# Two buffers of x change places in a fused attention and feed-forward kernel: which unit's x goes to the late pool

## The chip, the cores and the metric

The kernel runs on one core of one Trainium2 chip. The metric is the device time of one execution in microseconds: the median of several runs. Before the change it is 931.96 us, the median of three runs (930.52, 931.96 and 933.09). A profiled execution took 932.41 us; its span in the trace, on which all times below are counted, is 930.6 us.

## The reference

Linear attention without a softmax, a normalisation, and a feed-forward layer with a squared ReLU, all in fp32:

```python
# q, k, v: (8 batches, 8 heads, 576 rows, 64); g_norm: (64,)
kv = np.einsum('bhsd,bhse->bhde', k, v)
out = np.einsum('bhsd,bhde->bhse', q, kv)
rms = np.sqrt(np.mean(out * out, axis=-1, keepdims=True) + 1e-06)
out = out / rms * g_norm
x = out.transpose(0, 2, 1, 3).reshape(4608, 512)
# w_in: (512, 2048), w_out: (2048, 512), s and b: one number each
h = x @ w_in
r = np.maximum(h, 0.0)
g = s * (r * r) + b
return g @ w_out
```

## The kernel before, in words

**Units.** The 4608 rows of x are worked off in nine units (`u` from 0 to 8) of 512 rows. A unit has 512 rows times 512 features of x, kept transposed in one tile `xT[u]` (128 partitions, 2048 numbers each). A unit has two parts: the first product with its ReLU and square (`mm1`, four steps `s` of 512 columns of `w_in`), and the second product (`mm2`), whose results are stored. Meanwhile the attention for the next unit is done piece by piece between the matmuls: `attention_of_two` makes two blocks of 128 rows, so a unit needs two of them, `A` and `B`.

**Seven products instead of eight.** From unit 1 on, the products are done in Strassen's manner (the form of Winograd), so a block product becomes seven half-size products of sums and differences. The names `x1`, `z2`, `x6`, `y7`, `x5`, `x3`, `y4` give the bank of PSUM (x, y or z) and the number of the product. `x5`, `x3`, `x6` go on adding in the bank in which `x1` began, `y4` in the bank of `y7`. Products 1, 2 and 3 read `xT[u]` itself (`x_of`), products 4 to 7 read sums (`xs`). After `x5`, ScalarE copies the bank to r4 (`keep`), and VectorE adds y and r4 to `a22` and squares it. Product `y4` may add into its bank only when that addition has read it. `x3` and `y4` of a step come in the step after it; those of unit 1's last step (`s = 3`) come in slot 0 of `mm2(1)`, just after its first product, `x1(0)`.

**The order.** The order of the work is written out by hand, and each engine takes its instructions in this order: the tables in `sides` and `side_of` say ahead of which product, or in which slot of `mm2`, a piece of attention is put. For unit 1 the entry `(3, 2): [A["norm"], A["turn_x"]]` puts the normalisation (L584) and the transpose into `xT[2]` (L595) in the last step, ahead of `y7` and of `x5` with its addition. All matmuls of the products have the line of one helper, L91; additions and subtractions on VectorE have L251 and L254.

**The buffers of x.** `turn_x` in `attention_of_two` takes the tile for `xT[u]` from a pool when a unit's first two blocks come (`j == 0`). The pool `xp` has one buffer under this name from the beginning. The pool `late["x"]` has one more; it is made in `tc_late` at the end of unit 0, when the pool `convp`, with the weights of unit 0 and the raw tiles of their conversion, is given back, and it lies in that memory. In the kernel before, units 0, 1 and 2 all use the one buffer of `xp`; then units 3, 5 and 7 use the late one and units 4, 6 and 8 that of `xp`. A tile's first writing waits until all readers and writers of what lay there before are done; these waits are put in when the program is built. The readers of `xT[1]` are the products x1, z2 and x3 of unit 1 and the sums of unit 1's x (L254), and the last of them is x3 of the last step.

**Transfers.** SyncE issues most loads: k and v, a ring of seven buffers for weights of the second product (L789, L786, filled by `pump`) and, once, the 32 small loads of q for unit 3 (L1382). GpSimd issues the other loads of q (L1341), the stores of the output (L921) and, in `mm2(1)`, stores of sums of weights (L833, `parts_of_w`).

Of the kernel before, what the change touches and what calls it, by code (L numbers as in the profile page):

```python
# [16 lines left out]
def kernel(  # L17
# [61 lines left out]
    xp = ctx.enter_context(tc.tile_pool(name="xp", bufs=1))  # L79
# [40 lines left out]
    def parts(c):  # L120

        g, i = divmod(c, R)
        if g == 0:
            if i == 4:
                return [(0, 8, 1), (1, 8, 1)]
            b, i = (0, i) if i < 4 else (1, i - 5)
            return [(b, i, 1), (b, 4 + i, 1)]
        if i == 4:
            return [(2 * g, 16, 2), (2 * g + 1, 0, 2)]
        return [(2 * g, 4 * i, 4)] if i < 4 else [(2 * g + 1, 4 * i - 18, 4)]  # L130
# [268 lines left out]
    late, xT = {}, {}  # L399
# [12 lines left out]
    def small(name, n, i=""):  # L412
        return attp.tile([P, n], FP32, name=name, tag=f"{name}{i}")
# [85 lines left out]
    def scale_x(u, j):  # L499
        to = xT[u][:, :, j * P : j * P + 2 * P]  # L500
        for i in range(KC):
            nc.scalar.activation(to[:, i], to[:, i], AF.Copy, scale=g_col[:, i : i + 1])  # L502

    def attention_of_two(c):

        u, j = divmod(c, 4)  # L510
        by_block = []
        for i in range(2):
            p = parts(c + i)
            by_block += [p[0][0]] * 2 + [p[-1][0]] * 2
        runs = []
        for w, b in enumerate(by_block):
            if runs and runs[-1][0] == b:
                runs[-1][2] = 32 * w + 32
            else:
                runs.append([b, 32 * w, 32 * w + 32])  # L520
        W = 8
        st = {}

        def turn(i=None):
            if i in (None, 0):
                st["qT"] = attp.tile([P, 2 * DM], FP32, name="qT", tag="qT").rearrange(
                    "p (a x) -> p a x", a=NP
                )
            if i is None:
                nc.vector.transpose(  # L530
                    out=st["qT"], in_=q_tile[c].rearrange("p (a x) -> p a x", a=NP)
                )
                return
            to = st["qT"][:, :, i * P : i * P + P]
            if c + i >= R:
                nc.vector.transpose(out=to, in_=q_in[c + i])
                return
            ps = ps_t.tile([P, NP, P], FP32, name="qT_ps", tag="t")
            for p in range(NP):
                nc.tensor.transpose(ps[:, p, :], q_in[c + i][:, 2 * p : 2 * p + 2, :], ident)  # L540
            nc.scalar.copy(to, ps)

        def product():
            ps = [ps_t.tile([P, 2, 2 * P], FP32, name="y_ps", tag="t") for _ in range(2)]
            for b, lo, hi in runs:
                for r in range(2):
                    for p in range(NP):
                        for l in range(2):
                            rows = slice(l * HB, l * HB + HB)
                            at = l * HB + r * 32  # L550
                            nc.tensor.matmul(  # L551
                                ps[l][32 * p : 32 * p + 32, r, lo:hi],
                                lhsT=bd_kv[b % 2][rows, p, at : at + 32],
                                rhs=st["qT"][rows, p, lo:hi],
                                start=True,
                                stop=True,
                            )
            st["ps"] = ps

        def back():  # L560
            y = q_tile[c].rearrange("p (w l d) -> p w l d", w=W, l=2)
            for l in range(2):
                nc.vector.transpose(
                    out=y[:, :, l].rearrange("p w (r e) -> p r w e", r=2),
                    in_=st["ps"][l].rearrange("p r (w t) -> p r w t", w=W),
                )

        def square():
            st["xn"] = attp.tile([P, 2 * DM], FP32, name="xn", tag="xn")
            nc.scalar.activation(st["xn"], q_tile[c], AF.Square)  # L570

        def row_sum():
            st["ss"] = small("ss", 2 * W, 2)
            nc.vector.reduce_sum(
                st["ss"], st["xn"].rearrange("p (h d) -> p h d", d=D), axis=mybir.AxisListType.X
            )
            st["rms"] = small("rms", 2 * W, 2)
            nc.scalar.activation(st["rms"], st["ss"], AF.Sqrt, bias=eps_col, scale=1.0 / D)

        def norm():  # L580
            inv = small("inv", 2 * W, 2)
            nc.vector.reciprocal(inv, st["rms"])
            shape = (P, 2 * W, KC, D // KC)
            nc.vector.tensor_tensor(  # L584
                out=st["xn"].rearrange("p (c h e) -> p h c e", c=KC, h=2 * W),
                in0=q_tile[c].rearrange("p (h c e) -> p h c e", h=2 * W, c=KC),
                in1=inv.unsqueeze(2).unsqueeze(3).to_broadcast(shape),
                op=ALU.mult,
            )

        def turn_x():
            if j == 0:
                pool = late["x"] if u > 2 and u % 2 else xp
                xT[u] = pool.tile([P, KC, 2 * TB], FP32, name="xT", tag="xT")
            nc.vector.transpose(  # L595
                out=xT[u][:, :, j * P : j * P + 2 * P],
                in_=st["xn"].rearrange("p (c x) -> p c x", c=KC),
            )

        return dict(  # L600
            turn=turn, product=product, back=back, square=square, row_sum=row_sum, norm=norm,
            turn_x=turn_x, scale=lambda: scale_x(u, j),
        )

# [913 lines left out]
```

## Time and profile before

| | before |
|---|---|
| median of three runs | 931.96 us |
| span of the profiled execution | 930.6 us |
| TensorE, matmuls | 915.8 us busy, 7118 instructions |
| VectorE | 670.4 us busy, 1175 instructions |
| ScalarE | 196.5 us busy |
| GpSimd | 231.6 us busy |
| DMA | 165.79 MB, mean 178 GB/s |
| mean granted TensorE clock | 0.995 |
| transposes into xT at L595 | 16, 1242 ns each (median) |

How to read it: the lines of the profile give busy time by engine; PE is TensorE (PEld its weight loads, which overlap), DVE is VectorE, ACT is ScalarE, POOL is GpSimd, SP is SyncE. The list of waits has, for each pair of a waiting line and its releaser, the total wait in us, the number of waits and the longest. In the chain that ended last each piece of work is followed back to what released it. Times in a timeline are microseconds from the start of the span. The granted clock is the share of TensorE's full speed that the chip allowed in a stretch. The ends of matmuls are modelled in the profile and overlap, so the pace of a run of matmuls is taken from starts: sixteen matmuls of 128x256 take 3.45 us on the chain, eight take 1.73.

### The profile page before, as it was taken

Reading aid. Unit: us, or ns where it says so; the run is one execution under the profiler, and the core shown is the slowest. Engines: PE = TensorE matmul, PEld = TensorE weight load, DVE = VectorE, ACT = ScalarE, POOL = GpSimd, SP = SyncE. Lnnn points to the kernel's source line nnn. Section 1 sums busy time; section 2 is a strip of 40 time slices with the busy share of each in tenths; the row PEclk is TensorE's granted clock in tenths of the full one; section 3 lists DMA queues with packets and bytes.
Section 4 is the critical chain, followed back from the end, with each engine's and each line's share of the span. In section 5 each row is a group of like instructions: output and inputs, shape, how many; then the busy total and the mean of one; then the engine's idle time right before and its main releaser. Section 6 shows DMA issues by size and latency. Waiting matters only on the chain.

```text
span 930.6 us, 17540 instructions
## 1 busy us (share of the span) xinstructions
PE 915.8 (98%) x7118; PEld 826.7 (89%) x7118; DVE 670.4 (72%) x1175; ACT 196.5 (21%) x355; POOL 231.6 (25%) x426
## 2 busy tenths in 40 slices
PE   7999999999999999999999999999999999999997
PEld 6888888878889998899889988999899989998997
DVE  2789678676567886877777777787677867874585
ACT  2684122211023002310231013201330022001200
POOL 2000016215633152720264035603330300020000
PEclk9999999999999999999999999999999999999999
DMA  9587827349951694158514853377317800680075
GB/s 236 192 318 273 271 73 234 115 131 320 341 159 34 215 324 149 27 181 289 193 49 140 268 199 104 110 233 267 104 57 235 289 9 22 219 309 17 24 229 167
DMA packets 81376, 165.79 MB, mean 178 GB/s; under 512 B 25872, under 2 KB 34576, under 8 KB 81168
## 3 DMA queue, kind: packets, MB, share of 16 engines
q1 hardware_dynamic: 61872, 136.14, 44.4%
q0 software_dynamic: 15680, 25.98, 9.3%
q10 hardware_dynamic: 3744, 2.56, 1.1%
q8 instruction: 56, 0.92, 0.4%
q14 instruction: 24, 0.20, 0.1%
HBM read 136.84 MB, written 27.79 MB: 177 GB/s over the span
## 4 chain that ended last, share of the span: by engine, by line
PE 95%; DMA 2%; DVE 1%; ACT 1%; issue 0%; SPq 0%; ACTq 0%; DVEq 0%
PE x_ps L91 42%; PE y_ps L91 30%; PE z_ps L91 11%; PE t_ps L91 8%; PE y_ps L551 2%; PE kv_ps L381 2%; DMA w_raw<-in_moe_w_in_dram 1%; DMA kv_sb<-in_k_dram 1%; DVE sub L254 0%; ACT w_raw L231 0%; PE qT_ps L540 0%; ACT w_raw L226 0%; DVE xT L491 0%; DVE xn L467 0%; SPq L107 0%
## 5 line engine op out<-in xcount | busy, mean ns | idle before, releaser
L1341 POOL DMA_DIRECT2D q_sb<-in_q_dram x256 | 143.7, 569 | 141.4 <-issue 83.8
L921 POOL DMA_DIRECT2D out_dram<-o x110 | 54.7, 504 | 417.7 <-DVE o L251 257.2
L695 ACT COPY r<-x_ps 128x512 f32<-128x512 f32 x96 | 56.0, 584 | 448.0 <-PE x_ps L91 430.8
L91 PE MATMUL y_ps<-xs,wb 128*128 128x256 f32 x512 | 123.0, 383 | 1.9 <-DVE a L251 1.9
L91 PE MATMUL x_ps<-xs,ws 128*128 128x256 f32 x512 | 122.3, 382 | 0.0
L91 PEld LDWEIGHTS y_ps<-xs,wb 128*128 128x128 f32 x512 | 96.7, 191 | 16.0 <-DVE a L251 2.3
L91 PEld LDWEIGHTS x_ps<-xs,ws 128*128 128x128 f32 x512 | 96.2, 190 | 16.5 <-issue 3.8
L251 DVE TENSOR_TENSOR a<-y_ps,r 128x512 f32<-128x512 f32 x64 | 44.1, 689 | 87.2 <-ACT r L695 70.8
L91 PE MATMUL x_ps<-xT,wa 128*128 128x256 f32 x384 | 89.6, 380 | 0.1
L91 PEld LDWEIGHTS x_ps<-xT,wa 128*128 128x128 f32 x384 | 72.3, 190 | 10.2 <-ACT xT L502 0.5
L91 PE MATMUL y_ps<-w_sb,sub 128*128 128x128 f32 x560 | 69.5, 275 | 0.0
L91 PEld LDWEIGHTS y_ps<-w_sb,sub 128*128 128x128 f32 x560 | 66.4, 192 | 0.6 <-DVE r L817 0.2
L650 DVE SCALAR_TENSOR_TENSOR a<-a 128x512 f32<-128x512 f32 x89 | 61.5, 691 | 2.8
L91 PE MATMUL y_ps<-w_sb,a 128*128 128x128 f32 (+1 forms) x416 | 61.0, 295 | 0.0
L91 PE MATMUL x_ps<-xT,ws 128*128 128x256 f32 x256 | 60.5, 379 | 0.0
L91 PE MATMUL z_ps<-xT,wa 128*128 128x256 f32 x256 | 60.5, 379 | 0.0
L91 PE MATMUL x_ps<-w_sb,s 128*128 128x256 f32 x256 | 57.7, 379 | 0.0
L91 PEld LDWEIGHTS y_ps<-w_sb,a 128*128 128x128 f32 x416 | 55.5, 192 | 2.1
L91 PE MATMUL t_ps<-w_sb,sub 128*128 128x128 f32 x448 | 54.9, 275 | 0.5 <-DVE r L817 0.5
L91 PEld LDWEIGHTS z_ps<-xT,wa 128*128 128x128 f32 x256 | 48.6, 190 | 6.6
L91 PEld LDWEIGHTS x_ps<-xT,ws 128*128 128x128 f32 x256 | 48.1, 190 | 6.2
L91 PEld LDWEIGHTS t_ps<-w_sb,sub 128*128 128x128 f32 x448 | 52.3, 192 | 0.8 <-DVE r L817 0.7
(160 smaller groups left out, 1401.2 us busy)
## 6 DMA issues: line engine op xcount, KB each, us to landing
w_sb<-w SPq DMA_DIRECT2D x154, 512.0 KB, 4.7
w_sb<-w SPq DMA_DIRECT2D x42, 256.0 KB, 3.5
w_raw<-in_moe_w_in_dram SPq DMA_DIRECT2D x8, 1024.0 KB, 7.2
w_raw<-in_moe_w_out_dram SPq DMA_DIRECT2D x8, 1024.0 KB, 5.1
w_sb<-in_k_dram SPq DMA_DIRECT2D x24, 288.0 KB, 4.2
w_sb<-in_v_dram SPq DMA_DIRECT2D x24, 288.0 KB, 4.7
w<-sub POOLq DMA_DIRECT2D x24, 256.0 KB, 6.2
out_dram<-o POOLq DMA_DIRECT2D x92, 64.0 KB, 4.7
```

The costliest lines, as they stand in the source:

```text
L91: nc.tensor.matmul(o, lhsT=lhsT, rhs=rhs, start=start, stop=stop, skip_group_check=True)
L251: nc.vector.tensor_tensor(out=o, in0=a, in1=b, op=ALU.add)
L381: nc.tensor.matmul(ps[r][(r ^ l) * HB : (r ^ l) * HB + HB, i, :], lhsT=kv[l][rows, 0, j, :], rhs=kv[l][rows, 1, j, :], start=(j == 0), sto ...
L551: nc.tensor.matmul(ps[l][32 * p : 32 * p + 32, r, lo:hi], lhsT=bd_kv[b % 2][rows, p, at : at + 32], rhs=st["qT"][rows, p, lo:hi], start=Tr ...
L650: nc.vector.scalar_tensor_tensor(t, t, 0.0, t, ALU.max, ALU.mult)
L695: nc.scalar.copy(st[name], src)
L921: queues[s % 2].dma_start(out=view[b, jj, :, cols], in_=st[name, j][s * w : s * w + w, cols])
L1341: load()
```

## The change

One condition is turned over. The late pool's buffer is now used by the even units from unit 2 on, and the buffer of `xp` by units 0 and 1 and by the odd units from 3 on. It is meant so that the third unit's x doesn't have to wait for the buffer from which the second unit's products still read.

```diff
         def turn_x():
             if j == 0:
-                pool = late["x"] if u > 2 and u % 2 else xp
+                pool = late["x"] if u > 1 and u % 2 == 0 else xp
                 xT[u] = pool.tile([P, KC, 2 * TB], FP32, name="xT", tag="xT")
             nc.vector.transpose(
                 out=xT[u][:, :, j * P : j * P + 2 * P],
```

| unit | 0 | 1 | 2 | 3 | 4 | 5 | 6 | 7 | 8 |
|---|---|---|---|---|---|---|---|---|---|
| before | xp | xp | xp | late | xp | late | xp | late | xp |
| after | xp | xp | late | xp | late | xp | late | xp | late |

The two pools, their sizes and the order of the instructions stay as they are.

## The prediction

> **What bounds the kernel now.** I read the page from the top: busy shares, then the chain that ended last, then the places where TensorE sat idle, and last the stretch around the one place that the change touches.
>
> ```profile
> PE 915.8 (98%) x7118; PEld 826.7 (89%) x7118; DVE 670.4 (72%) x1175; ACT 196.5 (21%) x355; POOL 231.6 (25%) x426
> ...
> PE 95%; DMA 2%; DVE 1%; ACT 1%; issue 0%; SPq 0%; ACTq 0%; DVEq 0%
> ```
>
> TensorE is busy for 915.8 of 930.6 us and carries 95% of the chain. Only a gap in TensorE's own work can be worth anything. The waits of TensorE are these:
>
> ```profile
> PE y_ps L91 <- DVE a L251: 1.9, 1, 1.9
> PE kv_ps L381 <- DMA kv_sb<-in_v_dram: 1.5, 2, 0.8
> PE xT_ps L485 <- ACT w_raw L231: 1.4, 1, 1.4
> ```
>
> The longest is one wait of 1.9 us, at a y product, for an addition on VectorE; the other two lie before 30 us, where the change does nothing. Whose fault the addition's lateness is, the waits of VectorE tell:
>
> ```profile
> DVE xT L595 <- PE x_ps L91: 6.5, 1, 6.5
> ```
>
> The transpose that writes x of the third unit (L595) is one of 16 and the only one with such a wait: 6.5 us, for an x product of TensorE. The timeline of 176 to 226 us puts the two together; columns are start, duration, engine, line, operation, tiles, count, and in brackets the idle time before it with its releaser:
>
> ```profile
> 186.89 1.23 DVE L584 TENSOR_TENSOR xn<-q_sb,inv 128x1024 f32<-128x1024 f32 x1
> ...
> 189.22 3.62 PE L91 MATMUL x_ps<-w_sb,a 128*128 128x256 f32 x16
> 189.47 0.59 ACT L695 COPY r<-x_ps 128x512 f32<-128x512 f32 x1 [2.83 <-PE x_ps L91]
> 192.46 1.70 PEld L91 LDWEIGHTS x_ps<-xT,ws 128*128 128x128 f32 x8
> 192.67 1.89 PE L91 MATMUL x_ps<-xT,ws 128*128 128x256 f32 x8
> 194.60 0.60 ACT L730 ACTIVATE a<-x_ps 128x512 f32<-128x512 f32 x1 [4.54 <-PE x_ps L91]
> 194.60 1.25 DVE L595 STREAM_TRANSPOSE xT<-xn 128x1024 f32<-128x1024 f32 x1 [6.48 <-PE x_ps L91]
> 195.77 0.65 DVE L251 TENSOR_TENSOR a<-y_ps,r 128x512 f32<-128x512 f32 x1
> ...
> 196.47 3.21 PE L91 MATMUL y_ps<-xs,wb 128*128 128x256 f32 x8 [1.91 <-DVE a L251]
> ...
> 199.48 4.13 PE L91 MATMUL x_ps<-w_sb,a 128*128 128x256 f32 x16
> ```
>
> VectorE is done with the normalisation at 188.12 and then stands still: the old x lies in the buffer until its last reader, the x3 product of unit 1's last step, ends at 194.6. Behind the transpose in VectorE's queue stands the addition of `x5` (a22 = y + r4), whose inputs were both there at 190.06, when the copy of r4 ended. It is done only at 196.42, and product y4, which adds into the bank that this addition reads, waits for it. The last two rows show a second loss: eight matmuls of y4 took 3.21 us, where eight of the same kind elsewhere take 1.73 (chain of waits). Busy time by stretch, cut along the boundaries of the low clock (columns: stretch, its length, busy us and number of PE, PEld, DVE, ACT, POOL, granted TensorE clock, DMA share, GB/s):
>
> ```profile
> 190.27:193.68 3.41, 3.41 (x17) 3.00 (x17) 0.00 (x0) 0.00 (x0) 0.00 (x0) 1.00 0.33 51
> 193.68:197.10 3.42, 1.51 (x8) 1.00 (x7) 2.47 (x4) 1.82 (x5) 0.00 (x0) 1.00 0.34 51
> 197.10:200.51 3.41, 3.41 (x10) 2.66 (x9) 3.38 (x7) 0.49 (x2) 1.30 (x3) 0.50 0.20 45
> 200.51:203.92 3.41, 3.41 (x18) 3.00 (x17) 3.11 (x6) 0.00 (x0) 3.11 (x5) 1.00 0.96 313
> ```
>
> After a stretch in which TensorE was busy for 44% (1.51 of 3.42 us) the next 3.41 us ran at half clock: 10 matmuls instead of 17 or 18.
>
> **What the Trainium skill says.** "TensorE: Matmul & The Clock Gate", section "What's actually happening": the array's clock is halved after an idle window and given back after a busy one; the window is 3413 ns and free-running, so where it falls differs from run to run. The trace agrees on 3.41 us and on one half. The same page, "Why this matters for your kernels", warns of TensorE gaps over about 3 us; here a gap of 1.91 us was enough, so the measurement decides. "PSUM — Partial Sum Buffer", section "Engine vs sequencer instructions": VectorE's queue is strictly first in, first out, and matmuls keep program order. The trace agrees: an addition ready at 190.06 started at 195.77, directly after the transpose.
>
> **The change part by part.**
>
> *Removed: the wait of the third unit's first transpose.* It writes the late pool's buffer, which no earlier x used. The order of instructions on every engine stays the same. What replaces the semaphore of TensorE on this transpose are semaphores of DMA queues, since the late pool lies where the weights of unit 0 lay and these had to be stored first. The last of the weight stores was issued at 120.73 (timeline of the DMA queue), and they land in at most about 10 us (landing times of the stores from `w_dn`: 4.7 to 10.0). Even if it meant SyncE's later ring loads, the last of those before this point was issued by 163.3 (160.52 + 2.77); the longest landing in that stretch is 11.2. So all is done by 175, and the transpose at 188.1 finds no wait: cost nothing.
>
> *The new course.* Transpose 188.14 to 189.39 (1.25, its row). Addition a22 as soon as r4 is copied: 190.06 to 190.71. Squaring to 191.4. Then VectorE waits for the x1 product of the second half (end about 192.9), keeps r1 (0.48) and makes the four subtractions of weights (2.6 us) to 196.0; squaring, sum and difference of a21 take 2.1 more, to 198.1. TensorE: x3 ends its issue at 192.67 + 1.73 = 194.40; y4's bank was read by 190.71, so y4 starts at 194.40 with 3.7 us to spare, ends at 196.13, and x1(1), sixteen matmuls at 3.45 (chain: 3.45 for 16), ends at 199.58. Does a new wait arise? z2(0), next on TensorE, needs a12 of the last step only for its last quarter, from 199.58 + 2.6 = 202.2. VectorE gets there at 198.1 + 0.7 + 0.7 = 199.5. No wait.
>
> *The sum.* In the trace of before, z2(0) starts at 203.44; now at 199.58: **3.86 us less**. It splits into 1.91 of idle time, 3.21 - 1.73 = 1.48 on y4, and 0.5 on x1(1) (TensorE from 199.48 to 203.44 is 3.96 instead of 3.45): 3.89, the same within rounding.
>
> *Does it last to the end?* In both orders VectorE has caught up at the next r1 (before: it waits 0.19 us for TensorE there), so from z2(0) on the two engines stand to each other as before, 3.86 us earlier. What doesn't move with TensorE is SyncE's issue of 32 small q loads, from 188.25 to 205.1, as the normalisation that frees their buffer is not moved. Behind it stands the ring load of w2_7's second half, issued at 205.24, landing 4.4 us later at 209.6; product y7(0) reads it from about 218.64 - 3.86 + 0.9 = 215.7. Six microseconds to spare: hidden. GpSimd's stores of weight sums wait for the subtractions and move by 3.2 to 3.9 us with them. The tightest transfer of the next unit is its k and v, last issued at 242.73 with at most 8.6 to landing (251.3), used from 253.2: 1.9 us to spare; its issue waits for TensorE and for stores that follow VectorE, so it moves too, but perhaps not by all of 3.86.
>
> *Moved: all later units.* Unit 3 goes to the old buffer, unit 4 to the late one, and so on. Before, too, each shared with the unit two before it, and from unit 3 on no transpose at L595 shows a wait on a reader. Unit 3's new buffer was last read at 194.4, some 80 us before its write (281.9 in the trace before). Same instructions, same sizes: nothing.
>
> **The rivals.**
> (a) *The whole 3.86 comes* (forecast): 931.96 - 3.86 = 928.1.
> (b) *Only the idle time comes.* The low clock needs the free-running window to fall over the gap. In executions in which it falls otherwise, before has lost only the 1.91 us, and the gain is about 1.9: 930.0. For it speaks the spread of the three times (930.52 to 933.09), wider than anything else in the profile explains; against it, the profiled execution (932.41) had the low clock and is close to the median.
> (c) *The gain is given back* to a transfer that doesn't move: k and v for unit 2 with 1.9 us to spare, or the q loads for which VectorE already waits 2.0 us at 270.33. Of 3.86 us, 1.9 are hidden by the spare time, so up to 2 us could come back and bring a low clock of 1.7 with it: gain 0.2 to 2, 930.0 to 931.8. Against it: both queues wait for work that follows TensorE.
> (d) *Slower.* The transpose and the whole of VectorE's work now run under TensorE's x1, and a stall that I don't see, at the late buffer's DMA semaphores or in unit 3's buffer, makes a gap of 2 us with a low clock after it while nothing is won: 931.96 + 1.9 = 933.9. No row of the trace speaks for it.
>
> **How the numbers follow.** (a) 0.62, (b) 0.23, (c) 0.11, (d) 0.04. The predicted time is that of (a), 928.1. Executions of before lie within 1.3 us of their mean, and a median of a few within about 0.8. The low end is (a) less 1.2 us for that: 926.9; the high end takes in (b) with its 0.6: 930.6. Faster by over 0.3% means below 929.16: nearly nine tenths of (a), a good third of (b) by scatter or by a median in which the low clock was present, some of (c): 0.65. Within 0.3%: the rest of (a), (b) and (c), 0.31. Slower: 0.04.
>
> **What would show it.** After the change, the transposes at L595 have no wait on an x product; the wait of y_ps for `a` at L251 is gone from TensorE's list; the granted clock is 1.00 from 193 to 204; z2 of unit 1 starts near 199.6, and the last matmuls end 3.9 us earlier (923.61 less 3.9). Step by step it would be wrong if the first transpose waits for a DMA, if y4 still waits, if TensorE shows a new wait for kv or for a ring load after 205 us, or if the clock falls to half elsewhere.

## The result, and the profile after

The changed kernel takes 929.17 us (median of six executions, 927.05 to 930.6); the kernel before, run beside it, 932.69 us (six, 930.52 to 933.8). The ratio is 0.9962, with a 95% interval of 0.9946 to 0.9979: 3.5 us faster, and by the interval 2.0 to 5.0 us. The forecast was 928.1, which rested on a gain of 3.86 us from 931.96; beside the changed kernel, the kernel before was 0.7 us slower than that.

The same views as before, of the changed kernel. The page's busy times:

```profile
PE 912.7 (99%) x7118; PEld 824.7 (89%) x7118; DVE 670.2 (72%) x1175; ACT 196.5 (21%) x355; POOL 232.3 (25%) x426
```

The instructions are as many as before. TensorE's waits, the longest ones:

```profile
PE xT_ps L485 <- ACT w_raw L231: 1.5, 1, 1.5
PE warm_ps L91 <- POOL ident masks.py:199: 1.4, 1, 1.4
PE xT_ps L485 <- DVE xn L467: 0.8, 1, 0.8
PE kv_ps L381 <- DMA kv_sb<-in_v_dram: 0.7, 2, 0.4
```

The wait of y_ps for an addition at L251 is gone. These four lie before 31 us; behind that one wait of 0.5 us is left in the list. The timeline of the stretch around the change (start, duration, engine, line, operation, tiles, count, idle time before with its releaser):

```profile
185.59 1.22 DVE L584 TENSOR_TENSOR xn<-q_sb,inv 128x1024 f32<-128x1024 f32 x1
...
186.85 1.25 DVE L595 STREAM_TRANSPOSE xT<-xn 128x1024 f32<-128x1024 f32 x1
...
188.17 0.59 ACT L695 COPY r<-x_ps 128x512 f32<-128x512 f32 x1 [2.83 <-PE x_ps L91]
188.79 0.69 DVE L251 TENSOR_TENSOR a<-y_ps,r 128x512 f32<-128x512 f32 x1 [0.70 <-ACT r L695]
...
193.09 1.89 PE L91 MATMUL y_ps<-xs,wb 128*128 128x256 f32 x8
...
194.82 3.62 PE L91 MATMUL x_ps<-w_sb,a 128*128 128x256 f32 x16
...
198.28 3.62 PE L91 MATMUL z_ps<-w_sb,a 128*128 128x256 f32 x16
```

The transpose starts as soon as the normalisation ends, without a wait for the old x or for a DMA. The addition follows when r4 is there and ends at 189.48; y4 starts 3.6 us later, straight after x3. Eight matmuls of y4 take 1.73 us from start to start and sixteen of x1(1) 3.46.

For a measure that leaves out the start of the program, take the time from the start of the normalisation (L584) to the start of z2(0): before 203.44 - 186.89 = 16.55 us, after 198.28 - 185.59 = 12.69 us. The difference is 3.86 us, the sum of the prediction.

The span fell by more, from 930.6 to 925.2. The chain has the rest: the first x products that wait for ScalarE's scaling of x start at 34.12 instead of 35.42, 1.30 us earlier, in a part that the change doesn't touch. From z2(0) on (198.28 against 203.44) to the last y product (918.44 against 923.61) all stands 5.16 to 5.17 us earlier, which is 3.86 + 1.30. So nothing of the 3.86 us was given back in 720 us. Where the 1.30 us at the start come from, and that not every execution of the kernel before loses 3.86 us, the experiments show. That the median moved by 3.5 us and not by 3.86 needs no reason: both lie in the interval.

### The profile page after: what moved, and what is told of

Same layout as the page of the kernel before. It is cut to its first block, busy times and chain, and to the rows that moved or that the text cites. A ratio compares the mean times of both kernels' runs of the same rounds, so it can differ in the third digit from the quotient of the medians.

```text
span 925.2 us, 17541 instructions
## 1 busy us (share of the span) xinstructions
PE 912.7 (99%) x7118; PEld 824.7 (89%) x7118; DVE 670.2 (72%) x1175; ACT 196.5 (21%) x355; POOL 232.3 (25%) x426
## 4 chain that ended last, share of the span: by engine, by line
PE 95%; DMA 2%; DVE 1%; ACT 1%; issue 0%; SPq 0%; ACTq 0%; DVEq 0%
PE x_ps L91 42%; PE y_ps L91 30%; PE z_ps L91 11%; PE t_ps L91 8%; PE y_ps L551 2%; PE kv_ps L381 2%; DMA w_raw<-in_moe_w_in_dram 1%; DMA kv_sb<-in_k_dram 1%; DVE sub L254 0%; ACT w_raw L231 0%; PE qT_ps L540 0%; ACT w_raw L226 0%; DVE xT L491 0%; DVE xn L467 0%; SPq L107 0%
## 5 line engine op out<-in xcount | busy, mean ns | idle before, releaser
L251 DVE TENSOR_TENSOR a<-y_ps,r 128x512 f32<-128x512 f32 x64 | 44.1, 689 | 85.9 <-ACT r L695 69.9
```

Of the source, the lines that this page charges most:

```text
L251: nc.vector.tensor_tensor(out=o, in0=a, in1=b, op=ALU.add)
```

## The experiments

### The old buffers, with the transpose after its readers

The third unit's first transpose is put behind x3 and y4 of unit 1; the buffers are those of before.

```diff
-                (3, 2): [A["norm"], A["turn_x"]],
+                (3, 2): [A["norm"]],
...
-            0: [A["scale"]],
+            0: [A["turn_x"], A["scale"]],
```

> The old buffers, but the third unit's first transpose stands after x3 and y4 of unit 1 in VectorE's queue, so it never has to wait for the old x. Measured from the start of the normalisation (L584) in unit 1's last step to the start of z2(0): 16.55 us before, 12.69 after. Theory (the loss is what is queued behind the waiting transpose, not the place of the buffer): 12.7 us here too, no wait of y_ps for a, clock 1.00 in this stretch, time like the changed kernel's, about 3.5 us under the kernel before. Rival (the late pool's place itself, or units 3 to 8 in other buffers, bring the gain): 16.5 us, time as before.

```profile
185.69 1.22 DVE L584 TENSOR_TENSOR xn<-q_sb,inv 128x1024 f32<-128x1024 f32 x1
...
197.99 1.24 DVE L595 STREAM_TRANSPOSE xT<-xn 128x1024 f32<-128x1024 f32 x1
...
198.38 3.62 PE L91 MATMUL z_ps<-w_sb,a 128*128 128x256 f32 x16
```

The transpose runs 4.8 us after y4's start (193.20) and waits for nothing. From normalisation to z2(0) it took 198.38 - 185.69 = 12.69 us. Median 927.4 us (eight executions) against 930.54 for the kernel before beside it (fifteen), ratio 0.9963 (0.9951 to 0.9976): 3.1 us. All of the gain in the trace comes without moving any x to another buffer. So the place in the late pool and the swap of units 3 to 8 bring nothing that can be seen. Here both are gone, the wait and the work that stood behind it; the next experiment parts them.

### The wait kept, with the addition ahead of it

```diff
-                (3, 2): [A["norm"], A["turn_x"]],
+                (3, 2): [A["norm"]],
...
         if u > 1:
             second["rest"]()
             continue
+        if u == 1:
+            A["turn_x"]()
```

> The old buffers; the transpose stands directly behind the addition of a22 and its squaring, ahead of r1 of x1(0). It still waits for x3, for about 3.1 us, but y4 doesn't stand behind it. Theory: no gap of TensorE at y4; VectorE gets through the rest until the last quarter of z2(0) with 0.1 us to spare, so 12.7 to 13.2 us from normalisation to z2(0), and the time within 0.5 us of the changed kernel's. Rival (any wait of VectorE there costs TensorE in proportion to its length): 3.1 of 6.5 us of waiting, so some 1.8 us are lost: 14.5 us, time about 1.8 us under the kernel before.

The timeline shows the wait still there:

```profile
188.50 0.69 DVE L251 TENSOR_TENSOR a<-y_ps,r 128x512 f32<-128x512 f32 x1 [1.98 <-ACT r L695]
...
192.80 1.89 PE L91 MATMUL y_ps<-xs,wb 128*128 128x256 f32 x8
...
193.00 1.25 DVE L595 STREAM_TRANSPOSE xT<-xn 128x1024 f32<-128x1024 f32 x1 [3.09 <-PE x_ps L91]
```

VectorE stands still for 3.09 us on the old x, as expected, and yet y4 starts at 192.80, right after x3. From normalisation to z2(0) it took 197.98 - 185.29 = 12.69 us; z2(0) itself then waited a little for a12 (its sixteen matmuls took 3.56 us on the chain instead of 3.45). Median 926.88 us (eight), ratio 0.9958 (0.9945 to 0.9972). The rival that each us of VectorE's wait costs TensorE a share has fallen: 3.1 us of wait cost 0.1 us. The intervals of this run and of the changed kernel overlap, so no difference between the two can be seen.

### A delay added back: two, four and six transposes more

In the changed kernel the third unit's first transpose is done over and over; the output stays the same. N is 3, 5 or 7.

```diff
+            for _ in range(N if u == 2 and j == 0 else 1):
-            nc.vector.transpose(
+                nc.vector.transpose(
```

> The changed kernel with the third unit's first transpose done three times over: 2.5 us more of VectorE's time ahead of the addition. VectorE stands idle for 0.7 us there and y4 has 3.6 us to spare. Theory: nothing moves, 12.69 us from normalisation to z2(0), no wait of y4. Rival (each us of VectorE's delay there costs TensorE a part): 13.2 to 15.

> The changed kernel with the third unit's first transpose done five times over (four more, the same output): 5.0 us more of VectorE's time ahead of the addition, where y4 has 3.6 us to spare. Theory: y4 waits 1.4 us; the stretch from normalisation to z2(0) grows from 12.69 to about 14.1 us, and if a gap of 1.4 us already halves the clock, to 15.8 (open: the trace before has half clock after a stretch that was 44% busy and none after one of 78%; here it is 59% if the gap lies in one stretch). Rival (the gap alone never costs clock): 14.1.

> As the run before, with six more transposes: 7.5 us ahead of the addition. Theory: y4 waits 3.9 us, and half clock for at least one stretch of 3.41 us adds 1.7: 12.69 + 3.9 + 1.7 = 18.3 us from normalisation to z2(0), 20 if two stretches run at half clock. Rival (the gap alone): 16.6.

| more transposes | VectorE's added time | y4 later by | normalisation to z2(0) | half clock behind y4's wait |
|---|---|---|---|---|
| 0 (changed kernel) | 0 | 0 | 12.69 us | no |
| 2 | 2.55 us | 0 | 12.69 us | no |
| 4 | 5.12 us | 0.75 us | 13.53 us | no |
| 6 | 7.68 us | 3.31 us | 18.91 us | 6.83 us |

Added time is the duration of all transposes less 1.25 (3.80, 6.37 and 8.93 in the timelines). "Later" compares the start of y4 with the start of x3 before it, 1.73 us where nothing waits.

With two more nothing moved: 197.65 - 184.96 = 12.69. With four, my expectation of 14.1 was missed. I had forgotten the 0.70 us that VectorE stands idle ahead of the addition anyway, until r4 is there. The other 3.61 us are the time to spare of the changed kernel, from the addition's end (189.48) to y4's start (193.09). With both, 5.12 - 0.70 - 3.61 = 0.81 us of delay are expected; y4 came 0.75 us later, z2(0) 0.84. With six, 7.68 - 0.70 - 3.61 = 3.37 are expected, and y4 came 3.31 later. So VectorE has 4.3 us here in which its work is free; what goes beyond that delays y4 by as much, within 0.1 us. The run with six has something more, shown by busy time by stretch (columns as before: stretch, length, busy time and number of PE, PEld, DVE, ACT, POOL, granted clock, DMA share, GB/s):

```profile
191.65:195.06 3.41, 1.36 (x7) 0.85 (x5) 3.31 (x4) 0.60 (x1) 0.00 (x0) 1.00 0.32 50
195.06:198.48 3.42, 2.33 (x6) 1.88 (x7) 3.35 (x7) 1.71 (x4) 0.00 (x0) 0.50 0.17 25
198.48:201.89 3.41, 3.41 (x10) 2.69 (x9) 3.34 (x7) 0.00 (x0) 3.00 (x6) 0.50 0.58 198
201.89:205.30 3.41, 3.41 (x17) 3.02 (x16) 2.05 (x4) 0.00 (x0) 1.41 (x2) 1.00 1.00 291
```

Two stretches at half clock. Of 18.91 - 12.69 = 6.22 us, 3.31 are the wait; the low clock should cost half of its 6.83 us, less the 1.1 us in which TensorE still waited, that is 2.9, and 2.91 are left. My 20 us for two stretches had counted the low clock in full where TensorE was still waiting. The rival that the gap alone counts (16.6) has fallen.

### The kernel before, once more

> The kernel before, unchanged, profiled once more. Theory: the gap of 1.9 us at y4 is there in every execution, the low clock behind it only where a stretch of the clock's 3.41 us is less than about half busy, which depends on where the stretches fall. Either 16.5 us from normalisation to z2(0), with half clock behind the gap, or about 14.8 us with full clock. Rival (the low clock always follows the gap): 16.5 us.

This execution had the gap and no low clock. Its timeline:

```profile
185.30 1.22 DVE L584 TENSOR_TENSOR xn<-q_sb,inv 128x1024 f32<-128x1024 f32 x1
...
193.00 1.25 DVE L595 STREAM_TRANSPOSE xT<-xn 128x1024 f32<-128x1024 f32 x1 [6.48 <-PE x_ps L91]
...
194.88 1.99 PE L91 MATMUL y_ps<-xs,wb 128*128 128x256 f32 x8 [1.91 <-DVE a L251]
...
200.16 2.11 PE L91 MATMUL z_ps<-w_sb,a 128*128 128x256 f32 x9
```

The waits are the same to 0.01 us (6.48 and 1.91), but z2(0) comes 14.86 us after the normalisation instead of 16.55. Here the clock fell only behind the last matmuls, at 925.11; counted back from there in steps of 3.413 us, the stretches of the clock lie otherwise over the gap:

```profile
191.25:194.66 3.41, 1.72 (x8) 1.16 (x7) 1.66 (x2) 0.97 (x2) 0.00 (x0) 1.00 0.33 50
194.66:198.08 3.42, 3.20 (x15) 2.84 (x16) 3.35 (x7) 1.33 (x4) 0.51 (x1) 1.00 0.18 27
```

A little of the gap falls into the second stretch, the first is 50% busy, and the clock stays. So the gap itself costs 14.86 - 12.69 = 2.17 us, the low clock behind it 16.55 - 14.86 = 1.69, about half of a stretch, and the rival that it always follows has fallen. These two sizes come from one trace each.

### The changed kernel, once more, with a clock for each execution

> The changed kernel, unchanged, with a clock for each execution. Theory: in executions of the kernel before without any low clock (0.999) the time is about 2.1 us above the changed kernel's at 0.999; in those with two low stretches (0.994, 0.995) it is 5 us above. The median falls between, 3 to 3.5 us under the kernel before. Rival (the gain is 3.9 us in every execution): 3.9 us also between executions at 0.999.

Median 927.6 us (five executions, 926.88 to 927.95) against 930.46 for the kernel before (ten, 928.88 to 931.05); ratio 0.9966 (0.9952 to 0.9979). In this second profile of the changed kernel, too, it is 12.69 us from normalisation to z2(0) (186.52 to 199.21).

I call a stretch of 3.41 us at half clock a low stretch. One takes 0.0018 off the mean clock of an execution. The half clock behind the last matmuls takes 0.0004 to 0.002 more (0.7 to 3.6 us of the span in the ten traces). So a mean of 0.999 or 1.0 means no low stretch, and 0.994 or 0.995 means two; 0.996 to 0.998 can have more than one meaning.

Executions without a low stretch: 929.66 us before (mean of three), 927.43 after (mean of two). The difference is 2.23 us, as the theory has it. That it is so close to the 2.17 of the gap alone is luck, for the three lie 1.5 us apart. The seven executions of before at 0.996 or 0.997 have a mean of 930.73, 3.1 above the changed kernel's median. Among the executions of before with a clock on record, 0.994 and 0.995 came up in the first profile and in four of the fifteen beside the first experiments: mean of the four 932.25, against 929.34 for the six of the fifteen at 0.999. These 2.9 us are about what two low stretches take in the traces, 1.69 at the gap and 1.30 at the start. One of the fifteen does not fit: it took 932.83 us, and 0.997 leaves room for one low stretch only. The 5 us could be checked only across two sets of executions on two chips (932.25 - 927.43 = 4.8), and that is weak: the changed kernel without a low stretch took 928.28 and 929.18 us in the set of the result, 927.25 and 927.6 in this one. The rival, 3.9 us in every execution, has fallen by the second trace of before; the few executions agree.

The profile of this run shows where the chance at the start comes from. Here, as in the first profile of before, a stretch over the gaps of the start is less than half busy, and the next runs at half clock:

```profile
19.24:22.65 3.41, 1.55 (x13) 1.18 (x12) 2.41 (x7) 2.55 (x7) 0.00 (x0) 1.00 1.06 351
22.65:26.07 3.42, 3.42 (x42) 2.95 (x43) 2.23 (x4) 2.00 (x7) 0.00 (x0) 0.50 0.63 234
```

In the profile after, the boundaries fall at 20.50 and 23.92 and the stretch is 56% busy (1.90 of 3.42); the clock stayed. The first x products start at 35.05 us here and at 35.42 in the first profile of before, both with a low stretch at the start; without one they start at 34.12 in the profile after and at 33.83 in the second profile of before.

### Idle matmuls at the start

To get below the changed kernel's time, TensorE's gaps at the start are filled in it.

```diff
-    warm(7)
+    warm(10)
...
     turn_x[0]()
+    warm(5)
     turn_x[1]()
```

> The changed kernel, with eight idle matmuls (into a bank that nobody reads, as those already there) in TensorE's two gaps between 19.6 and 22.5 us. Theory: where the stretch over these gaps is less than half busy, the next runs at half clock and the start takes 1.3 us longer (35.42 before against 34.12 after in the two profiles); filling the gaps takes this away. So no low clock near 23 us in the profile, and a median 0 to 0.7 us under the changed kernel's. Rival (the start hangs on the load of w_in and on ScalarE alone): the same median, or later by the time of the idle matmuls.

No stretch at the start was below 80% busy from 14 us on, and the clock was full. But the median is 927.92 us (six, 926.67 to 929.01), against 927.6 for the changed kernel beside it; the ratio to the kernel before is 0.9973 (0.9962 to 0.9985). All six had a clock of 0.998 or 0.999, and still they lie 2.3 us apart. The two at 0.999, which had no low stretch, are 927.37 and 929.01, so at least 1.6 us of the spread are not the clock; what they are stays open. Nothing is gained that can be seen: this version is not better.

## Why the prediction was right

**The removed wait** cost nothing to take away: the transpose started 0.04 us after the normalisation's end, so the DMA semaphores that replaced TensorE's had been reached by then.

**The queue behind it** was the cause. Argued from one trace, it is now shown: with the wait kept and only the addition moved ahead of it, TensorE lost 0.1 us; with the old buffers and the transpose moved, nothing.

**The sum of 3.86 us** came out to the hundredth between the two profiles (16.55 to 12.69), and the clock of the changed kernel was 1.00 from 187.7 to 201.4. That the two profiles were the right pair for it is luck: the second trace of before would have given 2.17. That y4 would have 3.7 us to spare was right too (3.6). The split was off. The 1.91 us of idle time count from a modelled end; from starts, y4 came 3.80 us after x3 in both traces of before, 2.07 more than 1.73. And the prediction set y4's duration of 3.21 against 1.73 from start to start; from starts y4 took 196.47 to 199.48, 3.01 us, so it lost 1.28 and not 1.48. With 0.51 on x1(1) the sum is again 3.86. Without the low clock y4 took 1.83 (194.88 to 196.71), so the gap costs 2.07 + 0.10 = 2.17, and the low clock the other 1.69.

**To the end:** all 5.16 us at z2(0) are there at the last product. Of rival (c) a part came true without a price. VectorE's wait for q grew:

```profile
DVE qT L530 <- DMA q_sb<-in_q_dram: 3.6, 1, 3.6
```

In the list of before this wait was 2.0; in the second profiles it was 2.4 before and 2.8 after, so part of the growth is chance. These loads, and the last load of v (issued at 239.53 instead of 242.73, 3.2 us earlier where TensorE came 5.2 earlier), didn't move by all of it; that both queues follow TensorE was thus only partly right. TensorE's wait for k and v in the list above is that of the start; in unit 2 there was none.

**The weak step** is the weighing of (a) against (b), 0.62 to 0.23. I took the whole 3.86 us as what a median execution of before loses, since the one profile had the low clock. But (a) and (b) are two executions of one kernel, not two answers of which one is true, and the median of a set should lie between. It did: 3.5 us in the result, 2.9 beside the second profile of the changed kernel. That this mixture is why, is argued and not shown, for the intervals of both sets (2.0 to 5.0 and 2.0 to 4.5 us) hold 3.86 as well as 2.17. How often the low clock comes can be estimated from the traces: a stretch at about 48% busy was the limit (0.456 fell, 0.494 and 0.504 didn't), so 1.77 us of the gap must lie in one stretch of 3.41; with a gap of 1.91 that is so for (3.41 - 1.91 + 2 x 0.14) / 3.41 = 52% of all positions. The mean gain is then by this estimate 2.17 + 0.52 x 1.69 = 3.05 us. The clocks on record allow it, but don't test it well: of 25 executions of before, 9 had no low stretch (0.999) and 4 had two, so that between 4 and 16 had one at the gap, if the gap and the start are the only places, as in the traces.

## What to carry to other kernels

A wait on a free buffer is read from what stands behind it in the same queue, and for whom, not from its length: 6.5 us of waiting cost 2.2 or 3.9, 3.1 us cost 0.1, and moving one instruction did as much as moving the buffer. Where a gap of TensorE is priced, the low clock behind it is a second, separate term that comes in some executions only; how often it comes is worked out from where the gap can fall in a stretch, and not read from one trace. Two profiles that differ by more than the change explains are compared from one fixed instruction to another around the change.

## What the runs showed of the hardware that was not expected

In these traces the clock changes in fixed stretches of 3.41 us. In the first trace of before it fell at 23.02, 197.10 and 927.55 us, which is 51 and 214 times 3.413 apart, and the low clock at the first two lasted 3.41 each. What a stretch gets goes with TensorE's busy share in the stretch before. Busy shares of 34, 40, 42, 44 and 46% at full clock were followed by half clock; 49% (near the end of the run with four more transposes), 50, 56 and 58% and more were not. A gap of 1.9 us was thus enough or not, by where it fell. Coming back took more, as far as one case shows. With six transposes more, a stretch at half clock that was 68% busy was followed by another at half clock, and only one that was 100% busy by full clock; the four other low stretches inside a program were 97 to 100% busy, and full clock followed. The start of the program points the same way: in the run with idle matmuls a first stretch of 81% busy (0.71 to 4.12 us) was followed by one in which 18 matmuls took 3.42 us, 0.19 each; with the transpose behind its readers, a first stretch of 88% (0.95 to 4.37) was followed by 26 matmuls in 2.91 us, 0.11 each. There the records of the clock don't reach back far enough, so this is read from the pace of the matmuls alone, and two runs don't make a limit.
